# Another opening for a fused attention and soft mixture-of-experts kernel

## The chip, the cores and the metric

The kernel runs on one core of one Trainium2 chip. The metric is the device time of one execution in microseconds (us), the median of the runs shown. Engines are named as in the profile: PE is TensorE's matmuls and PEld its weight loads, DVE is VectorE, ACT is ScalarE, POOL is GpSimd, SP is SyncE, which issues every DMA of this kernel.

## What is computed

Causal attention with a decay over 8 batches and 8 heads, 576 positions of 64 elements each, and then a soft mixture of 8 experts with 4 slots each over the 4608 rows of 512 that the attention gives. All of it in float32:

```python
log_f = np.log(np.clip(f, 0.0001, 1.0))
cum = np.cumsum(log_f, axis=-1)
scores = scale * (q @ k.T) + cum[:, :, :, None] - cum[:, :, None, :]   # -1e9 above the diagonal
x = softmax(scores) @ v                    # heads side by side: 4608 x 512
logits = x @ phi                           # 4608 x 32
slot_input = softmax(logits, axis=0).T @ x
slot_out = relu(slot_input @ w1) @ w2      # by expert
out = softmax(logits, axis=1) @ slot_out
```

## The kernel before

The 64 heads are taken as 32 pairs (g = 0 to 31), head i = 2g + h. For each head TensorE makes the scores twice. `s1` (L211) makes them by query blocks, and `tops` (L224) on VectorE adds the causal mask and takes each row's maximum into a tile MT. The maxima are turned into rows and become an operand of the second pass: `s2` (L260, L261) makes the scores transposed, with the decays and the maxima subtracted by the matmul itself, and `expo` (L267) on ScalarE takes the exponential into PTS. `causal` (L275, L278) on GpSimd cuts the diagonal, `s3` (L295) multiplies by the values, `norm` (L310 to L315) on VectorE divides.

Operands stand in tiles used in rotation, three deep for RAW, WA and YA (index g % 3). Rows 0 to 63 of WA and YA hold k and q rounded to fp32r by ScalarE (`round_k` L165, `round_q` L170). Row 64 of WA holds the cumulated decay rounded, row 96 its remainder, row 97 of YA takes the maxima, and other rows of 64 to 97 hold constants 0, -1 and -8. `dup_k` (L180) and `dup_q` (L184) copy the rounded operands by DMA into WB and YB, where `low_k` (L190) and `low_q` (L195) on GpSimd put the remainders.

The instructions of each engine run in the order in which the program lists them; that order is written out by hand. Waits between engines are put in by the framework from what tiles are read and written. SP issues the DMAs in program order too, and waits before one where its source or target isn't free.

The opening (L480 to L632) does the following. It fetches the decays f of all 64 heads to `fx`, with the two heads of pair 0 once more on partitions 64 and 96 (L488, L489); clamps them on VectorE (L508), takes the logarithm (ACT L509), sums along the row (DVE L510), rounds to `fp` (DVE L512), and puts the rounded rows and remainders of pair 0 into WA[0] (ACT L526, DVE L515). The remainders of all heads are made on GpSimd (L516). Fills with constants stand ahead of it: GpSimd fills rows of WA and YA for n = 0 and 1 (L495 to L498), VectorE fills a tile of ones `fy` (L500), the PSUM tiles `ring` whole (L505) and parts of the PSUM tiles `pv` (`blank`, L283 and L284). `warm` (L477) is a number of matmuls on `fy` or `cs` whose result in ring[0] (columns 0 to 191) is never used. The decays of pair 1 go by DMA from `fp` into WA[1] (L528), those of the later pairs by way of a DRAM tile `cumd` (L571, `load_cum` L175). The constant rows of WA[1] and YA[1] are copied to WA[2] and YA[2] by DMA (L574, L575).

Then `first(i, n, busy)` makes group n of head i's scores, `busy` warm-up matmuls and the maxima. For pair 0 `first_parts` (L538) copies the maxima from MT into a tile `m2` (a view of LG), and `first_rows` turns them (TensorE L545) and copies them into YA[0] (ACT L548). `both(i, n)` is `s2` and `expo`. Heads 0 to 4 are begun in this way, and from pair 1 on the loop (L666) runs; in it each pair makes `s2` of its own two heads, `s1` of the heads three and four further on, and the transposes of X (`px`, L322) of the pair before. In the last pairs and after the loop come the experts; their weights are fetched from L112, one piece a pair from g = 4 on.

Of the kernel before, what the change touches and what calls it, by code (L numbers as in the profile page):

```python
# [62 lines left out]
def attn_softmoe(ctx: ExitStack, tc: tile.TileContext, qk, v, f, phi, w1, w2, cst, out):  # L63
# [454 lines left out]

    for h in range(2):
        round_k(0, h)  # L520
        round_q(0, h)
        dup_k(0, h, h + 1)
        dup_q(0, h, h + 1)
        if h == 0:
            for n in range(2):
                nc.scalar.copy(WA[0][64:65, S * n : S * n + S], fp[64 + 32 * n : 65 + 32 * n, 0:S])  # L526
# [2 lines left out]
    nc.scalar.activation(fin[:, 0:1], ones[:, 0:1], AF.Exp)
    for h in range(2):  # L530
        low_k(h)
        low_q(h)
    nc.gpsimd.memset(YA[2][0:64, :, 0:64].bitcast(F32), 0.0)
    nc.gpsimd.memset(one, -1.0)

    def first_parts(h):

        nc.vector.tensor_copy(m2[h][:, :, 1:2], MT[0][:, NBLK * h : NBLK * h + NBLK].rearrange("p (t o) -> p t o", o=1))  # L538
# [496 lines left out]
```

## Time and profile before

| | us |
|---|---|
| median of 3 runs | 412.54 |
| lowest and highest | 411.88, 413.23 |
| the profiled execution | 411.51 |
| span of the profiled execution, first to last instruction | 409.8 |

| engine | busy us | share of the span |
|---|---|---|
| PE | 384.8 | 94% |
| PEld | 335.9 | 82% |
| DVE | 287.2 | 70% |
| ACT | 256.3 | 63% |
| POOL | 259.0 | 63% |

The profile is one execution. Times in it count from the span's start. A row of a timeline gives start and length in us, the engine, the source line, the operation, the tiles written and read, the shape, and in brackets how long the engine had been idle before it and what ended that. SPq rows are DMA issues: they tell when SP issued a transfer, not when it landed.

### The profile page before, as it was taken

The page shows a single profiled execution, that of the slowest core. Times are in us where ns is not written, and L with a number is a line of the kernel's source. Part 1 is how long each engine was busy: PE and PEld are TensorE (multiplying, and loading weights), DVE is VectorE, ACT ScalarE, POOL GpSimd, SP SyncE. Part 2 cuts the span into 40 slices and gives each one's busy share as a digit, 9 for nine tenths or more (in the row PEclk, how much of TensorE's full clock was granted, in tenths as well). Part 3 has the DMA queues.
Part 4 walks back from the last instruction along what each step waited for, and adds up shares of the span by engine and source line. Part 5 has one row for each costly group of instructions (what it writes and reads, how often), then busy time and mean ns, then how long its engine had stood idle before and what let it go on. Part 6 is the DMA issues. An engine that isn't in the chain of part 4 may idle for free.

```text
span 409.8 us, 15121 instructions
## 1 busy us (share of the span) xinstructions
PE 384.8 (94%) x5841; PEld 335.9 (82%) x5841; DVE 287.2 (70%) x1134; ACT 256.3 (63%) x655; POOL 259.0 (63%) x347
## 2 busy tenths in 40 slices
PE   4779999999999999999999999999999989999990
PEld 4668999999999998999899899999999875444770
DVE  7768777879787977797779687877887544312661
ACT  5657787768686777677767686788775533010551
POOL 9675888777777777787778677877787610020000
PEclk9799999999999999999999999999999999999997
DMA  6556567677867787777777777677766699998798
GB/s 194 140 159 191 153 172 181 202 209 206 243 204 213 211 239 210 204 204 237 204 205 198 207 203 203 203 203 204 202 176 159 219 372 363 386 417 356 241 370 314
DMA packets 34524, 94.02 MB, mean 229 GB/s; under 512 B 4060, under 2 KB 8850, under 8 KB 34452
## 3 DMA queue, kind: packets, MB, share of 16 engines
q1 hardware_dynamic: 34452, 93.06, 73.5%
q8 instruction: 46, 0.75, 0.7%
q14 instruction: 26, 0.21, 0.1%
HBM read 63.93 MB, written 9.73 MB: 180 GB/s over the span
## 4 chain that ended last, share of the span: by engine, by line
PE 79%; DMA 8%; DVE 7%; ACT 3%; issue 1%; SPq 0%; DVEq 0%; ACTq 0%
PE pv L295 22%; PE ring L260 12%; PE s L211 11%; PE ring L261 11%; PE pv L322 4%; DMA RAW<-in_qk 3%; PE pv L888 3%; DVE s L224 3%; PE lg L360 2%; DMA out<-p 2%; PE pv L855 2%; PE ring L855 2%; PE ds L441 2%; DMA p<-in_w 2%; PE more L965 1%
## 5 line engine op out<-in xcount | busy, mean ns | idle before, releaser
L267 ACT ACTIVATE PTS<-ring 128x320 f32<-128x320 f32 (+2 forms) x256 | 119.7, 514 | 62.9 <-PE ring L261 36.9
L224 DVE CUSTOM_DVE_ANT_0 s<-s,mask 128x320 f32<-128x320 f32 (+4 forms) x320 | 137.5, 449 | 8.0 <-PE s L211 3.6
L260 PE MATMUL ring<-YA,WA 98*128 98x320 f32 (+4 forms) x384 | 122.9, 333 | 0.4 <-ACT YA L548 0.4
L261 PE MATMUL ring<-YB,WB 128*128 128x320 f32 (+4 forms) x384 | 111.2, 297 | 0.0
L295 PE MATMUL pv<-V,PTS 128*64 128x65 f32 x3200 | 104.5, 223 | 0.4 <-ACT mr L243 0.3
L211 PE MATMUL s<-WA,YA 97*128 97x288 f32 (+4 forms) x384 | 99.1, 314 | 5.2 <-DVE WA L515 2.2
L295 PEld LDWEIGHTS pv<-V,PTS 128*64 128x64 f32 x3200 | 99.7, 137 | 3.1 <-issue 1.2
L190 POOL TENSOR_TENSOR WB<-RAW,WB 64x576 fp32r<-64x576 f32 x64 | 90.9, 1420 | 5.9 <-DMA WB<-WA 0.7
L195 POOL TENSOR_TENSOR YB<-RAW,YA 64x576 fp32r<-64x576 f32 x64 | 89.5, 1416 | 3.2 <-ACT YA L170 0.7
L260 PEld LDWEIGHTS ring<-YA,WA 98*128 98x128 f32 (+1 forms) x384 | 70.4, 185 | 6.2 <-issue 2.1
L211 PEld LDWEIGHTS s<-WA,YA 97*128 97x128 f32 x384 | 63.7, 192 | 11.3 <-POOL YA L498 2.7
L261 PEld LDWEIGHTS ring<-YB,WB 128*128 128x128 f32 (+1 forms) x384 | 70.5, 184 | 0.0
L275 POOL TENSOR_SCALAR_AFFINE_SELECT PTS<-PTS 128x384 f32<-128x384 f32 x64 | 33.3, 521 | 35.4 <-ACT PTS L267 28.1
L224 DVE DVE_READ_ACCUMULATOR2_ANT MT<- 128x1 f32 x384 | 54.3, 141 | 0.0
L278 POOL TENSOR_SCALAR_AFFINE_SELECT PTS<-PTS 128x128 f32<-128x128 f32 (+1 forms) x128 | 31.3, 265 | 32.2 <-ACT PTS L267 29.8
L165 ACT CAST WA<-RAW 64x576 fp32r<-64x576 f32 x64 | 39.9, 669 | 17.0 <-DMA RAW<-in_qk 16.6
L322 PE MATMUL pv<-cs,X 128*128 128x128 f32 x155 | 42.8, 277 | 0.3 <-DVE X L315 0.2
L224 DVE CUSTOM_DVE_ANT_0 s<-s,mask,MT 128x288 f32<-128x288 f32 x64 | 33.7, 526 | 9.9 <-PE s L211 1.1
L170 ACT CAST YA<-RAW 64x576 fp32r<-64x576 f32 x64 | 40.0, 670 | 0.4
L310 DVE TENSOR_SCALAR rl<-pv 128x5 f32<-128x5 f32 x64 | 10.5, 164 | 34.9 <-PE pv L295 34.9
L315 DVE TENSOR_TENSOR X<-pv,rl 128x320 f32<-128x320 f32 (+1 forms) x65 | 31.5, 486 | 2.4 <-DMA YA<-mr 0.3
L346 ACT COPY XT<-pv 128x128 f32<-128x128 f32 (+1 forms) x124 | 28.6, 292 | 0.0
(208 smaller groups left out, 354.3 us busy)
## 6 DMA issues: line engine op xcount, KB each, us to landing
w<-in_w SPq DMA_DIRECT2D x46, 512.0 KB
RAW<-in_qk SPq DMA_DIRECT2D x31, 576.0 KB
V<-in_v SPq DMA_DIRECT2D x32, 325.0 KB
WB<-WA SPq DMA_DIRECT2D x31, 288.0 KB
YB<-YA SPq DMA_DIRECT2D x31, 288.0 KB
p<-in_w SPq DMA_DIRECT2D x7, 512.0 KB
out<-p SPq DMA_DIRECT2D x6, 512.0 KB
X<-in_w SPq DMA_DIRECT2D x4, 512.0 KB
```

The source lines that it names most:

```text
L165: nc.scalar.copy(WA[g % 3][0:64, S * h : S * h + S], RAW[g % 3][64:128, h])
L170: nc.scalar.copy(YA[g % 3][0:64, h, 64:640], RAW[g % 3][0:64, h])
L190: nc.gpsimd.tensor_tensor(t[0:64], RAW[g % 3][64:128, h], t[64:128].bitcast(F32), op=ALU.subtract)
L195: nc.gpsimd.tensor_tensor(YB[g % 2][64:128, h], RAW[g % 3][0:64, h], YA[g % 3][0:64, h, 64:640].bitcast(F32), op=ALU.subtract)
L211: nc.tensor.matmul(t[:, o : o + w], ya[0:97, h, 128 * blk : 128 * blk + 128], wa[0:97, j0 : j0 + w], start=True, stop=True)
L224: nc.vector.tensor_tensor_reduce(out=t[:, o : o + w], in0=t[:, o : o + w], in1=mask[:, m0 : m0 + w], scale=1.0, scalar=top if n == 3 else ...
L260: nc.tensor.matmul(o, wa[0:98, j0 : j0 + n], ya[0:98, h, 64 + i0 : 64 + i0 + w], start=True, stop=False)
L261: nc.tensor.matmul(o, wb[:, j0 : j0 + n], yb[:, h, i0 : i0 + w], start=False, stop=True)
L267: nc.scalar.activation(PT[i % 2][:, SEG_O[bank] : SEG_O[bank] + at], t[:, 0:at], AF.Exp, scale=0.125)
L275: nc.gpsimd.affine_select(d3, d3, pattern=[[0, 3], [1, 128]], compare_op=ALU.is_ge, fill=0.0, base=0, channel_multiplier=-1)
L295: nc.tensor.matmul(o[64 * u : 64 * u + 64, t, :], PT[i % 2][:, at : at + 64], V[:, g % 2, c, 65 * h : 65 * h + 65], start=(c == 0), stop=( ...
L322: nc.tensor.transpose(pm[:, 0:128], x[:, t, 128 * (p % 2) : 128 * (p % 2) + 128], ident)
```

## The change

- `f` is fetched by three DMAs: all 64 heads, head 0's row broadcast to partitions 64 to 95, and head 1's row to partition 96. The fill of `fx` on VectorE, which the second fetch waited for, is gone.
- The constant rows of index 0 are filled by GpSimd first; those of index 1 by VectorE (WA[1] rows 64 to 95), ScalarE (YA[1], two scaled copies of `fy`, which is 640 wide now) and, behind, GpSimd (the rest).
- `warm` has 8 matmuls instead of 6 and stands ahead of the fills of `ring`; of each ring tile only the corner of 64 partitions and columns 448 to 511 is filled.
- Pair 0's maxima are written straight into `m2`; `first_parts` is gone.
- Pair 0's head 0 is rounded, copied and split before head 1; GpSimd takes head 0's k remainder ahead of the remainders of the decays.
- Pair 1's operands (`load_qk(1)`) are asked for after head 0's copies instead of at the start; pair 2's (`load_qk(2)`) after head 1's copies instead of after pair 1's. The copies of the constant rows to WA[2] and YA[2] stand ahead of the loads of pair 1's decays into WA[1], and these ahead of `cumd` and `load_v(0)`.
- Warm-up matmuls between the first groups are placed otherwise: four behind the first group of head 1, three behind the transposes, none in its later groups.
- Pair 2 is rounded earlier (`round_k(2)` and `round_q(2)` among the groups of heads 1 and 3), `s3(0)` runs in one piece ahead of head 4's first group, and `norm(0)` stands between head 4's groups.

```diff
-WARM = (6, 1)
+WARM = (8, 1)
...
+    m2 = [LG[:, 32 * h : 32 * h + 10].rearrange("p (t c) -> p t c", c=2) for h in range(2)]
...
-            top = MT[g % 3][:, NBLK * h + blk : NBLK * h + blk + 1]
+            top = MT[g % 3][:, NBLK * h + blk : NBLK * h + blk + 1] if g else m2[h][:, blk, 1:2]
...
-    fy = WB[1][:, 0:S].bitcast(F32)
+    fy = WB[1][:, 0:640].bitcast(F32)
...
-    nc.vector.memset(fx[64:97], 1.0)
     nc.sync.dma_start(fx[0 : B * H], f)
-    nc.sync.dma_start(fx[64:97:32], f[0:2])
+    nc.sync.dma_start(fx[64:96], f[0:1].broadcast_to([32, S]))
+    nc.sync.dma_start(fx[96:97], f[1:2])
...
-    for n in range(2):
-        nc.gpsimd.memset(WA[n][64:96].bitcast(F32), 0.0)
-        nc.gpsimd.memset(WA[n][96:98].bitcast(F32), -1.0)
-        nc.gpsimd.memset(YA[n][64:98].bitcast(F32), -8.0)
-        nc.gpsimd.memset(YA[n][0:64, :, 0:64].bitcast(F32), 0.0)
-    load_qk(1)
     nc.vector.memset(fy, 1.0)
...
+    nc.vector.memset(fin, 1.0)
+    nc.scalar.activation(fin[:, 0:1], fin[:, 0:1], AF.Ln)
+    nc.gpsimd.memset(WA[0][64:96].bitcast(F32), 0.0)
+    nc.gpsimd.memset(YA[0][64:98].bitcast(F32), -8.0)
+    nc.gpsimd.memset(WA[0][96:98].bitcast(F32), -1.0)
+    nc.gpsimd.memset(YA[0][0:64, :, 0:64].bitcast(F32), 0.0)
+    nc.vector.memset(WA[1][64:96].bitcast(F32), 0.0)
+    for h in range(2):
+        nc.scalar.mul(YA[1][64:98, h], fy[64:98], -8.0)
+    warm(WARM[0], fy)
     for h in range(2):
         nc.vector.memset(m2[h], -8.0)
     for t in ring:
-        nc.vector.memset(t, 0.0)
+        nc.vector.memset(t[64:128, 448:512], 0.0)
     pvv = [blank(t) for t in pv]
-    warm(WARM[0], fy)
     nc.vector.tensor_scalar(fx, fx, 1e-4, 1.0, op0=ALU.max, op1=ALU.min)
     nc.scalar.activation(fx, fx, AF.Ln)
...
+    nc.gpsimd.memset(WA[1][96:98].bitcast(F32), -1.0)
+    for n in (1, 2):
+        nc.gpsimd.memset(YA[n][0:64, :, 0:64].bitcast(F32), 0.0)
+    nc.gpsimd.memset(one, -1.0)
+    round_k(0, 0)
+    round_q(0, 0)
     nc.vector.tensor_copy(fp[:, 0:S], fz)
     for h in range(2):
+        n, to = 64 + 32 * h, slice(S * h, S * h + S)
+        nc.scalar.copy(WA[0][64:65, to], fp[n : n + 1, 0:S])
+        nc.vector.tensor_tensor(WA[0][96:97, to], fz[n : n + 1], fp[n : n + 1, 0:S].bitcast(F32), op=ALU.subtract)
+    dup_k(0, 0, 1)
+    dup_q(0, 0, 1)
+    load_qk(1)
+    low_k(0)
     nc.gpsimd.tensor_tensor(fp[0 : B * H, S:], fz[0 : B * H], fp[0 : B * H, 0:S].bitcast(F32), op=ALU.subtract)
...
+    low_q(0)
+    round_k(0, 1)
+    round_q(0, 1)
+    dup_k(0, 1, 2)
+    dup_q(0, 1, 2)
+    nc.scalar.activation(fin[:, 0:1], ones[:, 0:1], AF.Exp)
+    low_k(1)
+    low_q(1)
+    load_qk(2)
+    nc.sync.dma_start(WA[2][64:98].bitcast(F32), WA[1][64:98].bitcast(F32))
+    nc.sync.dma_start(YA[2][64:98].bitcast(F32), YA[1][64:98].bitcast(F32))
     for c in range(2):
         nc.sync.dma_start(WA[1][64 + 32 * c : 65 + 32 * c].bitcast(F32), fp[2:4, S * c : S * c + S].bitcast(F32))
...
+    nc.sync.dma_start(cumd.rearrange("h c s -> h (c s)"), fp[0 : B * H].bitcast(F32))
+    load_v(0)
...
     for n in range(4):
         first(0, n, WARM[1])
-    first_parts(0)
+    first(1, 0, 4 * WARM[1])
+    next(r0)
+    warm(3 * WARM[1], cs)
     round_k(1)
-    first(1, 0, WARM[1])
-    next(r0)
     next(r0)
     round_q(1)
-    nc.sync.dma_start(cumd.rearrange("h c s -> h (c s)"), fp[0 : B * H].bitcast(F32))
-    load_v(0)
     dup_k(1)
-    nc.sync.dma_start(WA[2][64:98].bitcast(F32), WA[1][64:98].bitcast(F32))
-    nc.sync.dma_start(YA[2][64:98].bitcast(F32), YA[1][64:98].bitcast(F32))
     dup_q(1)
-    load_qk(2)
     load_cum(2)
-    first(1, 1, WARM[1])
-    first(1, 2, WARM[1])
+    first(1, 1)
+    first(1, 2)
     both(0, 0)
     first(1, 3)
-    first_parts(1)
...
     low_q(2)
+    round_k(2)
...
     load_qk(3)
+    round_q(2)
...
-    round_k(2)
-    round_q(2)
-    s3(0, None, 5)
...
+    s3(0)
+    first(4, 0)
     mturn(1, 1, 2)
     mrows(1, 1, 2)
...
-    s3(0, 5, None)
-    norm(0)
-    first(4, 0)
     first(4, 1)
     s3(1, None, 12)
     first(4, 2)
+    norm(0)
     first(4, 3)
```

## Rows read from the trace of the kernel before

**Rows 1.** Busy time of each engine in stretches of 10 us: start and end, length, then for PE, PEld, DVE, ACT and POOL the busy us and the number of instructions, then the granted TensorE clock (1 is 2.4 GHz), the busy share of the DMA engines, GB/s.

```profile
10.00:20.00 10.00, 7.21 (x33) 6.14 (x32) 7.43 (x23) 6.52 (x11) 6.81 (x7) 0.73 0.51 132
...
40.00:50.00 10.00, 10.00 (x181) 9.55 (x181) 8.32 (x36) 7.48 (x18) 8.32 (x12) 1.00 0.56 155
```

**Rows 2.** The chain of work that ended last, from 0 to 60 us, in order of time: start, us, engine, tile, line.

```profile
10.42 0.33 PE ring L477 x2
...
11.23 0.50 DVE s L224
...
14.38 1.07 DVE LG L538
15.49 1.23 PE ring L545 x5
...
16.96 0.64 PE ring L477 x2
...
31.02 0.52 PE s L211 x2
...
40.13 3.18 PE pv L295 x99
...
49.01 3.18 PE pv L295 x100
```

**Rows 3.** Timeline of the opening, 0 to 16 us, all engines. PE's f32 matmuls are two instructions each.

```profile
2.51 1.56 DVE L505 MEMSET ring<- 128x512 f32 x3
...
3.05 4.21 PE L477 MATMUL ring<-WB 128*128 128x192 f32 x12 [3.05 <-DVE ring L505]
...
4.15 0.11 DVE L283 MEMSET pv<- 64x64 f32 x1
...
4.49 1.05 POOL L495 MEMSET WA<- 32x1152 f32 x1
...
4.63 1.23 DVE L508 TENSOR_SCALAR PTS<-PTS 97x576 f32<-97x576 f32 x1
...
8.57 2.63 DVE L515 TENSOR_TENSOR WA<-PTS 1x576 fp32r<-1x576 f32 x2
8.66 1.92 POOL L516 TENSOR_TENSOR PTS<-PTS 64x576 fp32r<-64x576 f32 x1
...
14.01 1.39 POOL L190 TENSOR_TENSOR WB<-RAW,WB 64x576 fp32r<-64x576 f32 x1
```

**Rows 4.** Who waited for whom from 0 to 45 us: engine, line, whom it waited for, us in total, times, the longest.

```profile
PEld pv L295 <- ACT mr L243: 0.3, 1, 0.3
```

**Rows 5.** The same view for SP's own queue, 0 to 45 us.

```profile
SPq L245 <- DMA YA<-YA: 3.8, 1, 3.8
...
SPq L175 <- DMA WA<-WA: 1.5, 1, 1.5
```

**Rows 6.** Timeline of SP alone: the issues of the copies of the constant rows, of pair 2's and pair 3's operands, of pair 2's decays and of the maxima of head 2.

```profile
11.89 1.35 SPq L528 DMA_DIRECT2D WA<-PTS  x2
...
15.35 0.63 SPq L574 DMA_DIRECT2D WA<-WA  x1
16.03 0.70 SPq L575 DMA_DIRECT2D YA<-YA  x1
...
19.38 1.14 SPq L156 DMA_DIRECT2D RAW<-in_qk  x1
22.08 0.56 SPq L175 DMA_DIRECT2D WA<-cumd  x1
26.48 0.79 SPq L245 DMA_DIRECT2D YA<-mr  x1
...
28.70 0.43 SPq L156 DMA_DIRECT2D RAW<-in_qk  x1
```

**Rows 7.** Timeline from 14 to 50 us, all engines.

```profile
20.68 0.63 PE L211 MATMUL s<-WA,YA 97*128 97x320 f32 x2
...
28.20 1.39 PE L295 MATMUL pv<-V,PTS 128*64 128x65 f32 x40
...
29.05 1.24 ACT L165 CAST WA<-RAW 64x576 fp32r<-64x576 f32 x2 [2.21 <-DMA RAW<-in_qk]
...
32.88 1.25 ACT L165 CAST WA<-RAW 64x576 fp32r<-64x576 f32 x2 [1.17 <-DMA RAW<-in_qk]
...
34.13 0.47 PE L260 MATMUL ring<-YA,WA 98*128 98x448 f32 x1
...
34.91 0.49 DVE L315 TENSOR_TENSOR X<-pv,rl 128x320 f32<-128x320 f32 x1
...
35.46 0.14 PEld L322 LDWEIGHTS pv<-cs,X 128*128 128x128 f32 x1 [0.33 <-DVE X L315]
```

**Rows 8.** Busy time of each engine in shorter stretches, columns as in rows 1.

```profile
14.00:16.00 2.00, 0.51 (x3) 0.34 (x4) 1.90 (x7) 0.07 (x1) 1.91 (x2) 0.67 0.76 166
18.00:20.00 2.00, 2.00 (x8) 1.87 (x7) 0.77 (x3) 1.14 (x3) 0.00 (x0) 0.50 0.17 52
20.00:22.00 2.00, 2.00 (x14) 1.98 (x13) 1.47 (x8) 0.87 (x2) 0.52 (x1) 0.62 0.99 245
```

**Rows 9.** The page: the busy share of the DMA engines in 40 equal slices of the span, in tenths, and the shares of the whole chain by engine.

```profile
DMA  6556567677867787777777777677766699998798
...
PE 79%; DMA 8%; DVE 7%; ACT 3%; issue 1%; SPq 0%; DVEq 0%; ACTq 0%
```

More of the change, by code (lines that the diff above doesn't have):

```diff
@@ L482, in attn_softmoe @@
     fp = PT[1][0:lanes, 0 : 2 * S].bitcast(F32R)
-    fy = WB[1][:, 0:S].bitcast(F32)
+    fy = WB[1][:, 0:640].bitcast(F32)
     st["r", 0] = RAW[0]
-    nc.vector.memset(fin, 1.0)
-    nc.scalar.activation(fin[:, 0:1], fin[:, 0:1], AF.Ln)
-    nc.vector.memset(fx[64:97], 1.0)
     nc.sync.dma_start(fx[0 : B * H], f)
-    nc.sync.dma_start(fx[64:97:32], f[0:2])
+    nc.sync.dma_start(fx[64:96], f[0:1].broadcast_to([32, S]))
+    nc.sync.dma_start(fx[96:97], f[1:2])
     for h in range(2):
@@ L493, in attn_softmoe @@
     nc.sync.dma_start(cs, cst[:, 0:258])
-    for n in range(2):
-        nc.gpsimd.memset(WA[n][64:96].bitcast(F32), 0.0)
-        nc.gpsimd.memset(WA[n][96:98].bitcast(F32), -1.0)
-        nc.gpsimd.memset(YA[n][64:98].bitcast(F32), -8.0)
-        nc.gpsimd.memset(YA[n][0:64, :, 0:64].bitcast(F32), 0.0)
-    load_qk(1)
-    nc.vector.memset(fy, 1.0)
-    m2 = [LG[:, 32 * h : 32 * h + 10].rearrange("p (t c) -> p t c", c=2) for h in range(2)]
+    nc.vector.memset(fy, 1.0)
+    nc.vector.memset(fin, 1.0)
[8 more added lines that the diff above has]
+    warm(WARM[0], fy)
     for h in range(2):
@@ L504, in attn_softmoe @@
     for t in ring:
-        nc.vector.memset(t, 0.0)
+        nc.vector.memset(t[64:128, 448:512], 0.0)
     pvv = [blank(t) for t in pv]
-    warm(WARM[0], fy)
     nc.vector.tensor_scalar(fx, fx, 1e-4, 1.0, op0=ALU.max, op1=ALU.min)
     nc.scalar.activation(fx, fx, AF.Ln)
-    nc.vector.tensor_tensor_scan(fz, fy[0:lanes], fx, 0.0, ALU.mult, ALU.add)
+    nc.vector.tensor_tensor_scan(fz, fy[0:lanes, 0:S], fx, 0.0, ALU.mult, ALU.add)
+    nc.gpsimd.memset(WA[1][96:98].bitcast(F32), -1.0)
+    for n in (1, 2):
+        nc.gpsimd.memset(YA[n][0:64, :, 0:64].bitcast(F32), 0.0)
@@ L512, in attn_softmoe @@
+    nc.gpsimd.memset(one, -1.0)
+    round_k(0, 0)
+    round_q(0, 0)
     nc.vector.tensor_copy(fp[:, 0:S], fz)
     for h in range(2):
-        n = 64 + 32 * h
-        nc.vector.tensor_tensor(WA[0][96:97, S * h : S * h + S], fz[n : n + 1], fp[n : n + 1, 0:S].bitcast(F32), op=ALU.subtract)
-    nc.gpsimd.tensor_tensor(fp[0 : B * H, S:], fz[0 : B * H], fp[0 : B * H, 0:S].bitcast(F32), op=ALU.subtract)
[L519 to L526, printed above, removed]
+        n, to = 64 + 32 * h, slice(S * h, S * h + S)
+        nc.scalar.copy(WA[0][64:65, to], fp[n : n + 1, 0:S])
+        nc.vector.tensor_tensor(WA[0][96:97, to], fz[n : n + 1], fp[n : n + 1, 0:S].bitcast(F32), op=ALU.subtract)
@@ L527, in attn_softmoe @@
     for c in range(2):
         nc.sync.dma_start(WA[1][64 + 32 * c : 65 + 32 * c].bitcast(F32), fp[2:4, S * c : S * c + S].bitcast(F32))
[L529 to L538, printed above, removed]
+    nc.sync.dma_start(cumd.rearrange("h c s -> h (c s)"), fp[0 : B * H].bitcast(F32))
@@ L612, in attn_softmoe @@
     low_q(3)
-    round_k(2)
-    round_q(2)
-    s3(0, None, 5)
+    nc.vector.memset(LG[:, 128:256], -1.0e30)
+    nc.vector.memset(EX[:, 192:256], 0.0)
+    s3(0)
+    first(4, 0)
     mturn(1, 1, 2)
@@ L619, in attn_softmoe @@
     dup_k(2)
-    nc.vector.memset(LG[:, 128:256], -1.0e30)
-    nc.vector.memset(EX[:, 192:256], 0.0)
-    s3(0, 5, None)
-    norm(0)
-    first(4, 0)
     first(4, 1)
```

## The prediction

> **What bounds the kernel now.** I read the trace in four steps. First the busy time in stretches of 10 us [rows 1]: from 40 to 50 us TensorE is busy all the time, from 10 to 20 us 7.21 us of 10, at a mean granted clock of 0.73 of the full 2.4 GHz (the lower level is 1.2). So the loop over the pairs is bound by TensorE, and whatever moves the start of the loop moves the end by as much: the two marks of the loop, 40.13 and 49.01, lie 8.88 us apart [rows 2], a pair of TensorE work, with no wait in it that a shift could fill. Second the chain of waits up to there [rows 2], third the timeline of the opening [rows 3], fourth the waits and the transfers of SP's queue [rows 5, 6]. Three points carry the sum; I call them C, F and L. C is the end of the clamp of the decays (L508), 4.63 + 1.23 = 5.86 [rows 3]. F is the first score matmul of pair 1, the first that reads pair 1's decay rows, at 20.68 [rows 7]. L is the first transposed score matmul of the loop, at 34.13 [rows 7]. So F = C + 14.8 and L = F + 13.45.
>
> **C, the decays.** Before, VectorE reaches the clamp at 4.63 after its fills, the clamp takes 1.23 us, and GpSimd's fill at 4.49 runs until 5.54 [rows 3]; 5.86 - 5.54 = 0.32 us are left, a plausible run of 576 elements, so the clamp stood behind that fill. The change takes most of GpSimd's fills away from there: 1.05 + 1.2 + 1.05 + 0.2 and then 1.05 + 0.6 from 0.8 us on are over near 6 us. It also takes two thirds of VectorE's fills out: three of 128x512 (1.56 us) become three of 64x64 at 0.11 [rows 3].
>
> But it puts the warm-up matmuls ahead of these three fills, into the same PSUM bank as the first (columns 0 to 191 there, 448 to 511 here). Does the fill wait for them? In the trace the value matmuls of head 1, which write columns below 325 of a PSUM tile, wait 0.3 us for ScalarE's copy L243, which reads columns 325 and up of the same tile [rows 4]. So the order is kept by bank, not by column, and the fill waits for all eight matmuls. On VectorE's queue behind it: two fills, four of pv, the clamp, and so every decay. If it were kept by column, the clamp would come about 3 us earlier (a rival, below). The Trainium skill, PSUM — Partial Sum Buffer, section PSUM bank collisions raise a hardware error, speaks against the change here: two engines have to be kept apart on one bank and quadrant even at disjoint columns.
>
> The warm-up starts when the 640-wide ones are there: at 0.52 us for 512 elements (1.56 for three [rows 3]) 0.87 + 0.65 = 1.5 us. Before, twelve instructions took 4.21 us [rows 3], 0.35 each, sixteen then 5.6 us, to 7.1. If the clock rises halfway they go at 0.17 each (the pair at 10.42 in 0.33 us [rows 2]) and end at 5.8. I take 6.5. Then three fills (0.45 with their gaps), the four of pv (4.15 to 4.63, 0.48) and the clamp with GpSimd at rest, 0.32: C = 7.75, between 7.1 and 8.4. First term: **+1.9 us (+1.2 to +2.5)**.
>
> Other edits here cost nothing: the broadcast fetch replaces a fill and is one DMA issue more (0.6 us on SP), over by 2.5 us, long before 6.5; if VectorE came at 4 us, its landing would count. The two scaled copies on ScalarE (0.75 each) fit between the table load and the wait for the clamp.
>
> **From C to the first maxima.** Logarithm, scan, cast and the first difference follow as before; the maxima began at 11.23 [rows 2], C + 5.4. The second difference took 1.87 of the 2.63 us of the pair, since GpSimd's difference (8.66, 1.92 us) ran until 10.58 [rows 3]. After, GpSimd's next reading step waits for a copy through DMA that is issued at C + 1.4 and takes over 2 us, so the second difference runs free: 1.2 us saved, first maxima at C + 4.2. The copy of the maxima that is removed (14.38, 1.07 us [rows 2]) stood behind GpSimd's step at 14.01 that ended at 15.40 [rows 3]; another 1.07 saved. These 2.2 us bring head 0 forward, but not F, as follows.
>
> **F, pair 1's decay rows.** Before, SP loads these two rows (L528) at 11.89 and only then copies the constant rows of WA[1] and YA[1] to WA[2] and YA[2], at 15.35 and 16.03 [rows 6]. After, the two copies come first. The row loads write rows that the first copy reads, so they wait for its landing, and everything queued behind them on SP waits too: the store of the decays, V of pair 0, the copies of pair 1's operands, the decays of pair 2. That such a wait is made the trace shows: the store of maxima into YA[1] stood 3.8 us until the YA copy had landed, at 26.45, and the decays of pair 2 until the WA copy had, at 22.06 [rows 5, 6]. So the copies took 6.7 us and 10.4 us from their issue.
>
> They are slow because few DMA engines carry them: from 18 to 20 us the share is 0.17 of 16 engines and 52 GB/s [rows 8]; 153 KB at 52 GB/s is 2.9 us, the 170 KB of YA 3.3 us, one after the other. The Trainium skill, DMA: Bandwidth & Descriptors, section Why a DMA increments its semaphore by 16 and not by 1, gives the rule, which speaks against this change: the engines are the largest number up to 16 that divides the rows, 2 for 34 rows, always the lowest ones. By it the row loads (2 rows) use the same two engines; it would change the sum by the 3.3 us of the YA copy.
>
> Now in numbers from C, by the rows of each step: operand copies of head 0 are issued at C + 1.4 and C + 2.1, pair 1's operands at C + 2.65 (4.17 us before), head 1's copies at C + 4.7 and C + 5.4, pair 2's operands at C + 5.9, the WA copy at C + 6.4, the YA copy at C + 7.1. An operand load takes 4.2 us (28.70 to 32.88 [rows 6, 7]), so the engines come to the WA copy at C + 9 to C + 10, and it lands at C + 12 to C + 13.2 (6.7 after its issue gives C + 13.1). The row loads are issued then. If they are free of the YA copy they land in 2 us, C + 14.5; behind it at C + 15.4 to C + 17.8. I take the latter, since pair 2's operands, asked for at 19.38 behind the YA copy [rows 6], came only at 29.05, with ScalarE waiting 2.21 us for them [rows 7], 9.7 us where 4.2 do without such a copy ahead: F = C + 16.2. Second term: 16.2 - 14.8 = **+1.4 us (-0.3 to +3.0)**. TensorE would be there sooner: first maxima at C + 4.2, head 0's 3.1 (11.23 to 14.38), transposes 1.23 [rows 2] and their copies, 1.9, three groups of scores 1.5, in all C + 10.7; at half clock, where one warm-up takes 0.64 instead of 0.33 us [rows 2] and the transposes wait for five of them, near C + 15. It idles until F either way.
>
> **From F to L.** Before, head 4's scores start at 31.02, 10.3 us after F, because pair 2's operands came so late [rows 2, 7]. After, they are long there; what is late next is VectorE, whose maxima take 3.1 us a head [rows 2]: heads 2 and 3 end at F + 6.8. TensorE in between makes head 0's 50 value matmuls (40 took 1.39 us [rows 7], 1.75 in all), so head 4 starts at F + 7.2, 3.1 us sooner. Paid back: norm(0), three instructions with 0.49 the largest [rows 7], 0.93 in all, now stands between head 4's maxima, norm(1) behind them, and the transposes of X that waited 0.33 us [rows 7] wait about 1.4. Third term: **-2.0 us (-2.4 to -0.6)**, the last if TensorE's clock is low there.
>
> **Sum.** 1.9 + 1.4 - 2.0 = +1.3 us. The profiled run took 411.51 us with a span of 409.8, 1.03 below the median of 412.54; a shift of the loop applies to both, so 412.54 + 1.3 = **413.8 us**, +0.3%, which is about what a measurement of this kernel can tell from no change.
>
> **The rivals.** (1) The row loads are not held: the WA copy lands before C + 7, or tiles are tracked in a way that I misread. F is then set by TensorE at 18.5 to 22.8, and L = F + 11.4 is 29.9 to 34.2, say 32, 2.1 us sooner: 410.4 us. For it: the copies may run faster where no other transfer stands ahead of them; against: 6.7 and 10.4 us in the trace. (2) The fills are tracked by address: C is near 5, F near 21.2, L 32.6, so 411.0 us; against it stands the wait of [rows 4]. (3) Slower still: TensorE idles up to 5 us ahead of F. In the trace its clock fell in a stretch from 14 to 16 us in which TensorE was busy 0.51 of 2 us, and was back only between 20 and 22 us [rows 8]. If it falls ahead of F, the scores of heads 2 and 3 and the value matmuls (1.75 to 3.5 us) run at half clock: +1.5 to 2 us, 415.6 us; it decides where the granted clock at F is 0.5. (4) The opening moves, but the end doesn't: the last tenths show the DMA engines at 9 and more [rows 9], so the weights could set the end: 412.5 us. Against it: their loads are issued from the same loop, and DMA is 8% of the chain [rows 9].
>
> **How the numbers follow.** Forecast 0.45, rival (1) 0.17, (2) 0.08, (3) 0.17, (4) 0.13. The three terms at their low ends give 411.0, at their high ends 417.4, and hardly all at once; with (2), half of (1) and (3) the range is 410.6 to 416.0. Slower by over 0.3%: (3) and half of the forecast, some more from its upper bounds, 0.43. Faster: (1), part of (2), 0.2. Within: 0.37.
>
> **What would show it.** VectorE's first 64x64 fill starting when the last warm-up matmul ends, and the clamp ending past 7 us, show the first step right; a clamp before 6 us shows it wrong. SP's row loads issued over 4 us after the YA copy, and TensorE idle before pair 1's first scores, show the second. Head 4's scores about 7 us after them and a longer wait of the transposes of X show the third. If the rows land before TensorE asks for them, the prediction is wrong on the fast side.

## The result and the profile after

The changed kernel takes 415.25 us (median of 5 runs, 414.6 to 415.94) where the kernel before takes 412.54; the ratio is 1.0063, with a 95% interval of 1.0035 to 1.0091, so 1.4 to 3.8 us slower. The profiled execution took 414.94 us with a span of 413.2. The line numbers of the changed kernel are 2 higher in the helpers: `s1` is L213, `s2` L262 and L263, `tops` L226, `s3` L297, `expo` L269.

First the timeline of the opening after, as in [rows 3].

```profile
1.65 5.02 PE L479 MATMUL ring<-WB 128*128 128x192 f32 x16 [1.65 <-DVE fin L495]
...
6.76 0.26 DVE L509 MEMSET ring<- 64x64 f32 x3 [3.68 <-PE ring L479]
...
7.46 0.46 DVE L511 TENSOR_SCALAR PTS<-PTS 97x576 f32<-97x576 f32 x1
...
12.34 0.50 DVE L226 CUSTOM_DVE_ANT_0 s<-s,mask 128x320 f32<-128x320 f32 x1 [0.17 <-PE s L213]
```

The fill of ring stands 3.68 us until the last warm-up matmul has ended, and the clamp ends at 7.46 + 0.46 = 7.92. That is C, 2.06 us later than before. The first maxima start at C + 4.42.

SP's issues after, as in [rows 6]: the copies to WA[2] (L542) and YA[2] (L543), pair 1's decay rows (L545), pair 3's operands (L158). Then SP's waits, as in [rows 5].

```profile
14.59 0.71 SPq L542 DMA_DIRECT2D WA<-WA  x1
15.34 0.61 SPq L543 DMA_DIRECT2D YA<-YA  x1
21.43 1.23 SPq L545 DMA_DIRECT2D WA<-PTS  x2
...
33.07 0.43 SPq L158 DMA_DIRECT2D RAW<-in_qk  x1
```

```profile
SPq L545 <- DMA WA<-WA: 5.4, 1, 5.4
```

Busy time in stretches of 2 us, columns as in rows 1 (start and end, length, PE, PEld, DVE, ACT, POOL, granted clock, DMA share, GB/s).

```profile
18.00:20.00 2.00, 2.00 (x15) 1.93 (x12) 0.53 (x2) 1.70 (x4) 1.32 (x1) 1.00 0.13 53
20.00:22.00 2.00, 0.89 (x6) 0.62 (x4) 1.46 (x6) 1.45 (x4) 0.42 (x1) 1.00 0.12 52
22.00:24.00 2.00, 0.00 (x0) 0.00 (x0) 0.00 (x0) 0.00 (x0) 0.10 (x1) 0.78 0.22 74
24.00:26.00 2.00, 0.68 (x3) 0.71 (x4) 0.00 (x0) 0.00 (x0) 0.00 (x0) 0.50 0.97 234
26.00:28.00 2.00, 2.00 (x13) 1.66 (x13) 0.98 (x4) 0.60 (x2) 0.19 (x1) 0.50 1.01 291
28.00:30.00 2.00, 2.00 (x8) 1.87 (x8) 1.40 (x5) 1.97 (x4) 1.58 (x3) 0.51 0.33 73
```

The row loads are held 5.4 us, until 21.43, for the WA copy. From 18 to 22 us the DMA share is 0.12 to 0.13 of 16 engines, which is the work of two engines, at 52 GB/s: those that make the copies. From 22 to 24 us TensorE, VectorE and ScalarE do nothing at all. In this rest the granted clock falls, and it is 0.50 to 0.51, the lower level of 1.2 GHz, from 24 to 30 us.

The timeline further on, as in [rows 7]: F, head 4's first scores, L, ScalarE's rounding of pair 3, the transposes of X.

```profile
25.32 0.77 PE L213 MATMUL s<-WA,YA 97*128 97x320 f32 x2 [4.44 <-DMA WA<-PTS]
...
33.95 0.50 PE L213 MATMUL s<-WA,YA 97*128 97x320 f32 x2
...
37.32 0.47 PE L262 MATMUL ring<-YA,WA 98*128 98x448 f32 x1
...
38.65 1.24 ACT L167 CAST WA<-RAW 64x576 fp32r<-64x576 f32 x2 [3.76 <-DMA RAW<-in_qk]
...
39.35 0.33 PE L324 MATMUL pv<-cs,X 128*128 128x128 f32 x1 [0.78 <-DVE X L317]
```

F is at 25.32 (C + 17.4, before C + 14.8), with TensorE waiting 4.44 us for the row loads. L is at 37.32 (F + 12.0, before F + 13.45). But the shift is not over at L: ScalarE waits 3.76 us for pair 3's operands, and it has to round them before it goes on with the loop's exponentials. The chain of waits shows the place from which the loop runs evenly, the first long row of value matmuls; I call its start M.

```profile
22.11 2.97 DMA WA<-PTS
...
45.52 3.18 PE pv L297 x84
54.40 3.18 PE pv L297 x94
```

M is at 45.52, before at 40.13 [rows 2], 5.39 us later; the next pair follows 8.88 later in both. From M to the end of the span it is 413.2 - 45.52 = 367.7 after, 409.8 - 40.13 = 369.7 before.

### The profile page after: what moved, and what is told of

Read it like the earlier page. It is cut to its first block, busy times and chain, and to the rows that moved or that the text cites. A ratio compares the mean times of both kernels' runs of the same rounds, so it can differ in the third digit from the quotient of the medians.

```text
span 413.2 us, 15143 instructions
## 1 busy us (share of the span) xinstructions
PE 387.0 (94%) x5853; PEld 339.8 (82%) x5853; DVE 283.6 (69%) x1132; ACT 258.0 (62%) x657; POOL 255.1 (62%) x345
## 4 chain that ended last, share of the span: by engine, by line
PE 87%; DVE 4%; DMA 3%; ACT 2%; issue 1%; POOL 0%; DVEq 0%; ACTq 0%
PE pv L297 24%; PE ring L262 13%; PE s L213 12%; PE ring L263 12%; PE pv L324 4%; PE lg L362 3%; PE pv L890 3%; PE ring L479 2%; PE pv L857 2%; DMA out<-p 2%; PE ring L857 2%; PE ds L443 2%; PE more L967 1%; ACT PTS L269 1%; PE pv L236 1%
## 5 line engine op out<-in xcount | busy, mean ns | idle before, releaser
L269 ACT ACTIVATE PTS<-ring 128x320 f32<-128x320 f32 (+2 forms) x256 | 119.9, 514 | 63.5 <-PE ring L263 37.8
L226 DVE CUSTOM_DVE_ANT_0 s<-s,mask 128x320 f32<-128x320 f32 (+4 forms) x320 | 137.4, 448 | 15.1 <-PE s L213 10.7
L262 PE MATMUL ring<-YA,WA 98*128 98x320 f32 (+4 forms) x384 | 122.6, 332 | 1.2 <-ACT PTS L269 1.2
L263 PE MATMUL ring<-YB,WB 128*128 128x320 f32 (+4 forms) x384 | 111.1, 297 | 0.0
L213 PE MATMUL s<-WA,YA 97*128 97x288 f32 (+4 forms) x384 | 100.3, 318 | 9.3 <-DVE WA L527 4.9
L297 PE MATMUL pv<-V,PTS 128*64 128x65 f32 x3200 | 104.3, 223 | 0.6 <-ACT mr L245 0.6
L297 PEld LDWEIGHTS pv<-V,PTS 128*64 128x64 f32 x3200 | 99.6, 137 | 3.2 <-issue 1.2
L213 PEld LDWEIGHTS s<-WA,YA 97*128 97x128 f32 x384 | 64.9, 196 | 14.5 <-ACT WA L526 5.1
L262 PEld LDWEIGHTS ring<-YA,WA 98*128 98x128 f32 (+1 forms) x384 | 70.2, 184 | 7.1 <-issue 2.1
L263 PEld LDWEIGHTS ring<-YB,WB 128*128 128x128 f32 (+1 forms) x384 | 70.5, 183 | 0.0
L226 DVE DVE_READ_ACCUMULATOR2_ANT MT<- 128x1 f32 x372 | 52.7, 142 | 0.0
L226 DVE CUSTOM_DVE_ANT_0 s<-s,mask,MT 128x288 f32<-128x288 f32 x62 | 32.6, 526 | 9.2 <-PE s L213 0.5
```

Of the source, the lines that this page charges most:

```text
L213: nc.tensor.matmul(t[:, o : o + w], ya[0:97, h, 128 * blk : 128 * blk + 128], wa[0:97, j0 : j0 + w], start=True, stop=True)
L226: nc.vector.tensor_tensor_reduce(out=t[:, o : o + w], in0=t[:, o : o + w], in1=mask[:, m0 : m0 + w], scale=1.0, scalar=top if n == 3 else ...
L262: nc.tensor.matmul(o, wa[0:98, j0 : j0 + n], ya[0:98, h, 64 + i0 : 64 + i0 + w], start=True, stop=False)
L263: nc.tensor.matmul(o, wb[:, j0 : j0 + n], yb[:, h, i0 : i0 + w], start=False, stop=True)
L269: nc.scalar.activation(PT[i % 2][:, SEG_O[bank] : SEG_O[bank] + at], t[:, 0:at], AF.Exp, scale=0.125)
L297: nc.tensor.matmul(o[64 * u : 64 * u + 64, t, :], PT[i % 2][:, at : at + 64], V[:, g % 2, c, 65 * h : 65 * h + 65], start=(c == 0), stop=( ...
```

## The experiments

Each was timed beside the kernel before on the same chip; a ratio is the experiment's time over that kernel's, with its 95% interval in brackets. They come from several sessions, in which the median of the kernel before lay between 412.54 and 412.99 us. So medians from different sessions compare to a few tenths of a us.

**Row loads ahead of the copies.**

```diff
+    for c in range(2):
+        nc.sync.dma_start(WA[1][64 + 32 * c : 65 + 32 * c].bitcast(F32), fp[2:4, S * c : S * c + S].bitcast(F32))
     nc.sync.dma_start(WA[2][64:98].bitcast(F32), WA[1][64:98].bitcast(F32))
     nc.sync.dma_start(YA[2][64:98].bitcast(F32), YA[1][64:98].bitcast(F32))
-    for c in range(2):
-        nc.sync.dma_start(WA[1][64 + 32 * c : 65 + 32 * c].bitcast(F32), fp[2:4, S * c : S * c + S].bitcast(F32))
```

> The changed kernel with one edit: the loads of pair 1's decay rows stand ahead of the copies of the constant rows to WA[2] and YA[2]. Theory (the row loads wait for the copy, and that alone holds pair 1's first scores): the row loads are issued near 15, right after GpSimd's remainders, and land before 18; pair 1's first scores start when TensorE has ended head 0's exponent scores, near 20.9 in place of 25.3, and the first long row of value matmuls in the loop near 41 in place of 45.5. If all of it reaches the end, 415.25 - 4.4 = 410.9 us, with some 2 us given back later 413. Rival (the two rows are slow for another reason, behind pair 2's operands): they land after 22, the scores start after 23, and the time is 414 to 415.3.

Measured: 416.89 us, ratio 1.0106 [1.0082, 1.013]. The timeline:

```profile
20.32 0.40 PE L213 MATMUL s<-WA,YA 97*128 97x320 f32 x2
...
30.10 0.57 SPq L177 DMA_DIRECT2D WA<-cumd  x1
30.16 0.87 ACT L269 ACTIVATE PTS<-ring 128x448 f32<-128x448 f32 x2 [6.15 <-issue]
...
31.75 1.41 POOL L192 TENSOR_TENSOR WB<-RAW,WB 64x576 fp32r<-64x576 f32 x1 [9.27 <-DMA WB<-WA]
```

The first half of the theory holds: F is at 20.32 and TensorE does not wait there. The second half falls: M is at 46.12, later still, and the time is no better. GpSimd now waits 9.27 us for the copy of pair 1's operands (`dup_k(1)`, which stood behind the copies of the constant rows before the edit too, but is now issued while they still run). ScalarE idles 6.15 us (its row names no releaser), and pair 2's decays are asked for at 30.10. The granted clock is 0.50 from 26 to 36 us, TensorE having rested from 26 to 30. The order on SP chose who stands behind the copies.

**Fills ahead of the warm-up.**

```diff
-    warm(WARM[0], fy)
     for h in range(2):
         nc.vector.memset(m2[h], -8.0)
     ...
     pvv = [blank(t) for t in pv]
+    warm(WARM[0], fy)
```

> The changed kernel with one edit: the warm-up matmuls stand behind the fills of ring and pv again, as in the kernel before. Theory (the clamp is late because the fill of ring waits for the warm-up, and everything up to pair 1's scores follows the clamp): the clamp ends near 4.3 in place of 7.9, pair 1's first scores start 17.4 later as before, near 21.7, and the value matmuls of the loop near 41.9; 411.6 us if it reaches the end whole, 413.7 with 2 us given back. Rival (the copies set pair 1's scores, whenever the clamp ends): the clamp is as early, but the scores stay past 24 and the time within 1 us of 415.25.

Measured: 415.28 us, ratio 1.0061 [1.0041, 1.0081], the same as with the change whole. From the timeline and the waits:

```profile
3.85 0.53 DVE L511 TENSOR_SCALAR PTS<-PTS 97x576 f32<-97x576 f32 x1
...
22.14 0.77 PE L213 MATMUL s<-WA,YA 97*128 97x320 f32 x2 [6.76 <-DMA WA<-PTS]
```

```profile
ACT WA L167 <- DMA RAW<-in_qk: 4.4, 2, 4.2
```

C is at 4.38 and F at 22.14, each within half a microsecond of the theory, but M is at 44.31 where the theory gave 41.9: ScalarE stands 4.2 us for pair 3's operands, and the granted clock was 0.50 from 20 to 26 us, having fallen while TensorE waited its 6.76 us (it was low once more, 0.58 and 0.56, from 40 to 44 us). Of 3.5 us gained at C, 1.2 were left at M and none can be measured at the end.

**Both edits.**

> The changed kernel with both edits. Theory (the two costs add up): the clamp ends near 4.3, pair 1's first scores start near 17 to 18, the value matmuls of the loop near 37 to 38, some 3 us sooner than in the kernel before (40.13); if the end follows whole, 407.5 us, if transfers later in the loop hold it at a time of their own, 410.5 to 412.5. Rival (one hides the other): no better than the better of the two alone.

Measured: 412.91 us, ratio 1.0008 [0.999, 1.0025], the same as before. Together they give 2.3 us, alone nothing: the time does not add up from C and F. F is at 15.20, 5.5 us ahead of the kernel before, and M at 42.80. The waits say who took it:

```profile
POOL WB L192 <- DMA WB<-WA: 13.2, 2, 10.8
```

Again GpSimd waits 10.8 us for pair 1's operand copy, which is issued while the copies of the constant rows still occupy two engines. The granted clock is 0.50 or little more from 24 to 34 us, so the wait and the clock behind it share what is lost.

**A pure delay.**

```diff
+    warm(32, cs)
     for g in range(1, NG):
```

> The kernel before with 32 warm-up matmuls more right ahead of the loop over the pairs, 32 x 0.164 = 5.25 us of TensorE and nothing else. It asks how much of a shift of the loop reaches the end. Theory (in the kernel before some pairs wait for operands whose transfers keep a time of their own, so a later loop waits less): the first pairs are 5.3 us later, the end 3.0 to 3.5 us, 415.7 us. Rival (the waits seen in that one trace are chance, or move with the loop): the end is 5.3 us later, 417.8 us.

Measured: 422.27 us, ratio 1.023 [1.0193, 1.0267]. I had mis-costed the delay: 0.33 us is one warm-up, of two instructions, so 32 are 10.7 us.

```profile
34.38 10.67 PE L477 MATMUL ring<-cs 128*128 128x192 f32 x64
```

M moved by 10.36 us to 50.49, the span by 8.0, and the median by 9.5 (from 412.81). Between the two traces 2.4 us are taken up later, about the 2 that the theory gave back; by the medians it is only 0.9. The delayed kernel's own executions lie between 419.18 and 423.53 us, and the profiled one, 419.49, is among its fastest. So most of a shift reaches the end, and how much comes back is left open by this run.

**The copies split.**

```diff
-    nc.sync.dma_start(WA[2][64:98].bitcast(F32), WA[1][64:98].bitcast(F32))
-    nc.sync.dma_start(YA[2][64:98].bitcast(F32), YA[1][64:98].bitcast(F32))
+    for a, z in ((64, 96), (96, 98)):
+        nc.sync.dma_start(WA[2][a:z].bitcast(F32), WA[1][a:z].bitcast(F32))
+    for a, z in ((64, 96), (96, 98)):
+        nc.sync.dma_start(YA[2][a:z].bitcast(F32), YA[1][a:z].bitcast(F32))
```

> The changed kernel with one edit: each copy of the constant rows to WA[2] and YA[2] is made as two, 32 rows and 2 rows, in place of one of 34 rows; the order on SP stays, with two issues more (1.3 us). Theory (34 rows go over two DMA engines only, and whatever is queued on those two behind them is late; 32 rows spread over all 16, like the 64-row operand copies that land in 2.1 us): the copies land within 3 us of their issue in place of 6.8, the row loads are issued near 18.5 in place of 21.4 and land near 20.5 in place of 25; pair 1's first scores start near 21, the value matmuls of the loop near 40.5 in place of 45.5, and the time is 410.5 to 412. Rival (the copies are slow because of what stands ahead of them, pair 2's operands, not because of the engines they use): they land after 20.5, the scores start past 24, and the time stays within 1 us of 415.25.

Measured: 412.89 us, ratio 1.001 [0.9981, 1.0039], 2.4 us better than the change. SP's issues, and the stretches:

```profile
15.04 1.36 SPq L543 DMA_DIRECT2D WA<-WA  x2
16.45 1.19 SPq L545 DMA_DIRECT2D YA<-YA  x2
20.49 1.27 SPq L547 DMA_DIRECT2D WA<-PTS  x2
```

```profile
18.00:20.00 2.00, 2.00 (x16) 1.82 (x15) 0.00 (x0) 0.91 (x3) 1.72 (x2) 1.00 0.64 156
20.00:22.00 2.00, 1.65 (x11) 1.34 (x9) 1.62 (x6) 2.00 (x5) 0.00 (x0) 1.00 0.02 5
```

Both were partly right. The stretch in which only two engines work is gone: 0.64 of the engines are busy from 18 to 20 us, 0.02 after that. But the row loads are released only 0.9 us sooner (20.49); that the split copies now stand behind pair 2's operands on all engines would explain it and was not tested. F comes to 23.01, with 1.36 us of waiting. M is at 43.00; the granted clock, 1.00 at F, was 0.50 from 38 to 40 us.

**The copies split, and the fills ahead.**

> The same split copies, and the fills of ring and pv ahead of the warm-up. Theory (the clamp and the two clogged DMA engines are the whole loss, and add up): the clamp ends near 4.4, pair 1's first scores start near 17.5, nobody waits over 3 us for the operand copies of pair 1, and the value matmuls of the loop start near 36.5, 3.6 us before those of the kernel before; 408.5 to 410 us. Rival (something else then sets the loop's start, pair 3's operands, which are asked for behind the maxima of head 2): the value matmuls past 38.5, 411 us.

Measured: 411.51 us, ratio 0.9965 [0.9947, 0.9983]. C is at 4.38, F at 18.88, M at 42.37: the rival holds. The chain of waits:

```profile
26.65 7.28 DMA RAW<-in_qk
```

Pair 3's operands, asked for at 26.65 (behind the maxima of head 2, V of pair 1 and phi), take 7.28 us, and ScalarE waits 6.31 us for them.

**Pair 3's operands sooner, on top.**

```diff
     load_cum(2)
+    load_qk(3)
 ...
-    load_qk(3)
```

> The changed kernel with the split copies, the fills ahead of the warm-up, and one edit more: pair 3's operands are asked for right behind the load of pair 2's decays, in place of behind the maxima of head 2, V of pair 1 and phi. In the run without this edit ScalarE waited 6.3 us for them, issued at 26.65 and landed at 34, while the DMA engines had stood nearly still from 24 to 26. Theory (the request comes too late): issued near 21.5, landed near 27, ScalarE waits under 1 us, the value matmuls of the loop start near 38 in place of 42.4, and the time falls from 411.5 to 407.5 to 409. Rival (between 26 and 36 all 16 DMA engines are busy, so the same bytes end at the same time in any order): pair 2's or pair 4's operands or V are late in their place, the value matmuls past 41, the time within 1 us of 411.5.

Measured: 407.78 us, ratio 0.9889 [0.9864, 0.9914]. SP's issue of pair 3's operands:

```profile
22.32 0.87 SPq L158 DMA_DIRECT2D RAW<-in_qk  x1
```

M is at 38.22, and ScalarE's longest wait for operands is 0.3 us. The theory holds: one line moved is worth 3.7 us by the medians, 3.1 by the ratios to the kernel before (the run without it is from another session).

**The row loads ahead, on top of that.**

> The same kernel with the loads of pair 1's decay rows ahead of the four copies. Theory (with copies that are quick the order matters little for what stands behind them, and pair 1's scores gain the 3.5 us for which TensorE waited): pair 1's first scores near 15.5 in place of 18.9; the value matmuls of the loop near 36.5; 1 to 2 us less than the kernel beside it. Rival (the copies come 2 us later and hold pair 2's decays, and what sets the loop's start is pair 3's operands): no difference over 0.7 us.

Measured: 408.02 us, ratio 0.9891 [0.9873, 0.991]. F is at 15.51 in place of 19.68, M at 37.66 in place of 38.22: the rival. Four microseconds at F are worth nothing that can be measured. TensorE is busy only 0.52 of 2 us from 22 to 24 us here, and the granted clock is 0.50 or little more from 22 to 28.

**Parts alone in the kernel before.** The split copies, and nothing of the change:

> The kernel before with the split copies and nothing else of the change. Theory: the operands of pair 2 land near 25 in place of 29, ScalarE does not wait 2.2 us for them, and the value matmuls of the loop start near 38 in place of 40.13; 410.5 us. Rival (the wait for pair 2's operands was covered by VectorE's maxima): within 0.7 us of the kernel before.

Measured: 408.15 us, ratio 0.988 [0.9857, 0.9903]. ScalarE's two waits for operands in [rows 7], 2.21 and 1.17 us, became these:

```profile
25.16 1.24 ACT L165 CAST WA<-RAW 64x576 fp32r<-64x576 f32 x2
...
30.66 1.25 ACT L165 CAST WA<-RAW 64x576 fp32r<-64x576 f32 x2 [2.85 <-DMA RAW<-in_qk]
```

SP's issue of pair 2's load:

```profile
19.36 0.59 SPq L156 DMA_DIRECT2D RAW<-in_qk  x1
```

Pair 2's load is issued when it was before (19.36, before 19.38 [rows 6]), and its operands are rounded at 25.16 without waiting, in place of 29.05. M is at 37.53, and the time falls by more than the theory said, 4.8 us. With pair 3's operands sooner as well:

> The kernel before with the split copies and pair 3's operands asked for right behind the load of pair 2's decays. With the split copies alone it took 408.15 us. Theory (transfers that are asked for too late set the start of the loop there too): ScalarE's next wait for operands goes, the value matmuls of the loop start near 36.5 in place of 37.5; 407 us. Rival (VectorE's maxima set it there): within 0.7 us of 408.15.

Measured: 407.89 us, ratio 0.9891 [0.9866, 0.9916], M at 36.57. The trace agrees with the theory, the time with the rival: 0.3 us is no difference that these runs can tell. And with one part of the change in addition, maxima written where they are turned:

```diff
-            top = MT[g % 3][:, NBLK * h + blk : NBLK * h + blk + 1]
+            top = MT[g % 3][:, NBLK * h + blk : NBLK * h + blk + 1] if g else m2[h][:, blk, 1:2]
...
-    first_parts(0)
...
-    first_parts(1)
```

> The kernel before with the split copies, pair 3's operands asked for sooner, and one part of the change: pair 0's maxima are written straight where they are turned, so that the two copies of 1.07 us (L538) are gone. In the run without this part the chain of waits up to 30 us is VectorE's, and the first copy stands on it (14.37 to 15.44). Theory (a cut on that chain reaches the loop): the value matmuls of the loop start near 35.5 in place of 36.6, the time falls by 1 us from 407.9 to about 406.9. Rival (the operands of pairs 2 and 3, or TensorE, are late next by as much): within 0.5 us of 407.9.

Measured: 406.14 us, ratio 0.9837 [0.9802, 0.9872], the lowest median of all; M is at 35.49, 1.08 us sooner than without this part, and the span 1.4 us shorter. The theory holds in the trace. By the medians it is 1.75 us, but the two runs are from different sessions and the intervals of their ratios overlap. In the run without it its chain of waits held the copy:

```profile
14.37 1.07 DVE LG L538
```

**The kernel before, a second time.**

> The kernel before itself, once more with a profile, to tell what of its trace is chance. In its first trace the loop lost 2.1 us between 160 and 250 us to operand loads that came late, and the kernels with a later start lost less there. If these waits belong to the kernel's own timing, the second trace shows them again, 1.5 us or more; if they are chance, they are elsewhere or gone, and the span moves with them.

One run: 413.57 us, span 411.9. Its chain, and the stretches where it differs from the first trace:

```profile
19.38 9.83 DMA RAW<-in_qk
...
43.01 3.18 PE pv L295 x84
```

```profile
28.00:30.00 2.00, 0.54 (x20) 0.40 (x14) 0.85 (x3) 0.77 (x2) 1.28 (x1) 1.00 0.77 218
30.00:32.00 2.00, 0.72 (x5) 0.51 (x6) 0.25 (x1) 1.88 (x4) 0.77 (x1) 1.00 0.77 249
32.00:34.00 2.00, 2.00 (x30) 1.66 (x32) 1.64 (x9) 0.90 (x2) 2.00 (x2) 0.66 0.12 47
34.00:36.00 2.00, 2.00 (x27) 1.88 (x28) 1.21 (x8) 1.59 (x3) 0.01 (x1) 0.50 1.03 200
36.00:38.00 2.00, 2.00 (x9) 1.90 (x9) 1.42 (x5) 0.98 (x2) 0.00 (x0) 0.50 0.83 173
```

ScalarE's rounding of pairs 2 and 3 in it:

```profile
29.23 1.24 ACT L165 CAST WA<-RAW 64x576 fp32r<-64x576 f32 x2 [3.44 <-DMA RAW<-in_qk]
...
33.10 1.24 ACT L165 CAST WA<-RAW 64x576 fp32r<-64x576 f32 x2 [1.22 <-DMA RAW<-in_qk]
```

M is at 43.01, 2.9 us later than in the first trace of the same kernel, though F is 0.8 sooner (19.92). The operands do not make the difference: pairs 2 and 3 are rounded at 29.23 and 33.10, in the first trace at 29.05 and 32.88 [rows 7]. TensorE did little from 28 to 32 us, waiting for pair 2's operands, and its granted clock then fell to 0.50. In the first trace it was busier from 28 to 30 (1.59 of 2 us), and the clock stayed at 1.00. From head 4's first scores to M it is 11.80 us here (31.21 to 43.01) and was 9.11 there (31.02 to 40.13), nearly the whole 2.9 us.

The granted clock at the start of a trace needs care. In the first trace it was low from 14 to 22 us [rows 8]; in the second it reads 1.00 from 10 to 20 us, yet a warm-up matmul's two instructions take as long there as in the first trace at 0.50 (first row: the second trace; second row: the first trace). So TensorE was slow there in both.

```profile
16.75 0.84 PE L477 MATMUL ring<-cs 128*128 128x192 f32 x2
...
16.76 0.84 PE L477 MATMUL ring<-cs 128*128 128x192 f32 x2
```

From M to the end it is 368.9 us, and 369.7 in the first trace. TensorE idles 0.4 us between 160 and 240 us here, 1.0 in the first trace. That is below the 1.5 us that were to show these later waits again, so they are chance in the main. The larger chance is in the opening itself.

The marks of the profiled runs side by side (us; M from the chain of waits, F from the timeline):

| kernel | C | F | M | span | span - M | median |
|---|---|---|---|---|---|---|
| before, two traces | 5.86, 5.86 | 20.68, 19.92 | 40.13, 43.01 | 409.8, 411.9 | 369.7, 368.9 | 412.54 |
| changed | 7.92 | 25.32 | 45.52 | 413.2 | 367.7 | 415.25 |
| rows first | 7.68 | 20.32 | 46.12 | 414.6 | 368.5 | 416.89 |
| fills first | 4.38 | 22.14 | 44.31 | 412.3 | 368.0 | 415.28 |
| both | 4.38 | 15.20 | 42.80 | 410.7 | 367.9 | 412.91 |
| before, delayed | 5.87 | 20.70 | 50.49 | 417.8 | 367.3 | 422.27 |
| split | 8.39 | 23.01 | 43.00 | 411.6 | 368.6 | 412.89 |
| split, fills | 4.38 | 18.88 | 42.37 | 410.5 | 368.1 | 411.51 |
| split, fills, pair 3 sooner | 4.37 | 19.68 | 38.22 | 406.4 | 368.2 | 407.78 |
| the same, rows first | 4.45 | 15.51 | 37.66 | 406.3 | 368.6 | 408.02 |
| before, split | 5.86 | 19.28 | 37.53 | 406.0 | 368.5 | 408.15 |
| before, split, pair 3 sooner | 5.86 | 18.38 | 36.57 | 405.1 | 368.5 | 407.89 |
| the same, maxima in place | 5.86 | 17.30 | 35.49 | 403.7 | 368.2 | 406.14 |

The end follows M, 367.3 to 369.7 us behind it in all fourteen traces: from the earliest M to the latest it is 15.0 us, and the spans of these two differ by 14.1. It follows F much less: with F between 19.2 and 20.8 us, M lies anywhere from 37.5 to 50.5 (46.1 without the delayed kernel).

## Why the prediction was right, and where it was off

The sign was right and the time lies in the range; the forecast's 413.8 was 1.4 us low. That the time came so near is partly luck: the three terms measured sum to +3.2 at L in place of +1.3, a fourth loss of 2.2 us was not in the sum, and the median moved by only 2.7.

**C, +1.9.** Measured +2.06, by the mechanism named: the 64x64 fill starts when the last warm-up matmul has ended. The clamp with GpSimd at rest took 0.46 us, not the 0.32 worked out. Rival (2) falls. But as a term of the sum it was over-valued. With the fills put back, C and F come 3.5 and 3.2 us sooner and the time stays at 415.28; only with the row loads moved as well does it count. The prediction laid C, F and L in one series; pair 3's operands run beside them.

**F, +1.4.** Measured 17.4 - 14.8 = +2.6, inside the bounds of -0.3 to +3.0. The copy released the row loads at C + 13.5 (13.1 worked out), and they landed at 25.08, C + 17.2 (15.4 to 17.8 worked out). Their last step in the chain is 2.97 us long here and 1.68 in the same kernel with the copies split, so the YA copy in their way cost about 1.3 us. Rival (1) falls. That the wait is real is shown by moving the row loads ahead: it disappears. That it costs what it lasts is refuted by the same run, 416.89 us. What costs is two DMA engines that are busy for some 7 us with the copies; in the orders tried something stood behind them, and the step "F later, so the loop later" failed. The Trainium skill, DMA: Bandwidth & Descriptors, section Why a DMA increments its semaphore by 16 and not by 1, gives the cause in the number of rows: 2 engines for 34 rows and 16 for 32. The traces agree, with 0.12 to 0.13 of 16 engines from 18 to 22 us for copies of 34 rows, and with copies of 32 no such stretch: 0.64 from 18 to 20 us and 0.02 after that.

**F to L, -2.0.** Measured 12.0 - 13.45 = -1.45. Head 4's scores came at F + 8.6 (7.2 worked out, 10.3 before): pair 2's operands were there, as said, but heads 2 and 3 were made at the lower clock until 30 us. The transposes of X waited 0.78 in place of 0.33 us, less than the 1.4 feared for `norm(0)`.

**The copies are no cost of the change alone.** They slow both kernels. Split, they take 4.8 us off the kernel before and 2.4 off the changed one, and the changed kernel is then 4.7 us slower in place of 2.7 (412.89 against 408.15). With the fills ahead and pair 3's load moved as well, both kernels come out alike, 407.78 and 407.89. So what the change itself costs, once the copies are quick, is the fills and pair 3's late load, and the rest of it gains nothing that these runs can tell.

**What the sum did not have.** After L another 2.2 us are lost up to M (37.32 to 45.52 is 8.20, before 34.13 to 40.13 is 6.00), while ScalarE waits 3.76 us for pair 3's operands. The granted clock is 1.00 from 30 us on, so this is not the clock. Their load stands on SP behind the store of head 2's maxima, so the late F delays it too: 33.07 in place of 28.70 [rows 6]. The prediction took L for the start of the loop and listed every DMA that SP was held from up to pair 2's decays, not this one, four issues further. That moving this load matters is shown by the run in which it alone was moved (3.7 us by the medians), in a kernel in which the copies were split and the fills put back; in the changed kernel as it stands it was not moved alone.

**What came back.** Four terms make 2.06 + 2.58 - 1.45 + 2.20 = 5.39, the shift of M; the span grew by 3.4 and the median by 2.7. Between M and the end 2.0 come back. Of these, 1.0 is idle time of TensorE between 160 and 240 us, which the first trace of before has and the changed kernel does not; the prediction's "no wait in it that a shift could fill" holds for the pair that it looked at, not for the whole loop. Whether a later start fills such waits or chance does is not settled: the second trace of before has 0.4 there. The trace on which the sum was made weighs more: the second trace has M at 43.01, and against that the change's M is 2.5 us later, close to the medians. Rival (4) falls as well, since the delay moved the median by 9.5. The prediction's step that one execution's F and L stand for the kernel was the weakest one: between two traces of one kernel, where the clock fell moved M by 2.9 us.

**Rival (3).** Its condition, a granted clock of 0.5 at F, was met: TensorE rested from 22 to 24 us and ran at 0.50 or 0.51 from 24 to 30. But its price was not borne out where it was put: F to L came out 0.55 us above the forecast, not 1.5 to 2, and the 50 value matmuls ran at a granted clock of 1.00 (from 32.4 us, 1.66 us). So that 415.25 lies near its 415.6 is chance. What the clock alone costs was not isolated; the split copies in the changed kernel remove the rest and the low clock at F together and give back 2.4 us, with a low clock from 38 to 40 us in their place. Nor was `norm(0)` tried in its old place. The gain of the maxima written in place was hidden where something else was late: put into the kernel before with the transfers out of the way, the same edit brings M 1.08 us forward (407.89 to 406.14 us by the medians).

## What to carry to other kernels

Find the first place from which the work runs evenly and judge an opening by that mark alone, in more than one trace; waits that disappear ahead of it are no gain until it moves. Before moving a DMA in a queue, look at how many DMA engines carry it: here a slow transfer on two engines delayed the wide transfers behind it, and the order chose which, so make it wide (32 + 2 rows for 34 took 4.8 us off the kernel before) before thinking of the order. And follow a queue past the moved instruction to the last load that the steady work needs, not only to the first that waits.

## What the runs showed of the hardware

- Two copies of 34 rows split into 32 + 2 made a difference of 4.8 us in the kernel before, though SP issues two transfers more. Whole, they kept two of 16 DMA engines busy at 52 GB/s; a load issued behind them at the same time (19.38 and 19.36 us) was rounded at 29.05 us with the copies whole and at 25.16 with them split. In the changed kernel with both edits GpSimd waited 10.8 us for a 64-row copy behind them.
- The same kernel with the same opening reached M at 40.13 and 43.01 us; the recorded stretches of low granted clock lay from 14 to 22 us in one trace and from 32 to 40 in the other, TensorE having been busy 0.51 of 2 us where it began in the one, and 0.54 and 0.72 of 2 us ahead of it in the other. That alone makes a single trace a poor base for terms of 1 or 2 us.
- The granted clock read 1.00 at the start of the second trace while a warm-up matmul took 0.84 us at 16.75 us, as long as at 0.50 in the first trace (16.76 us). Durations of like matmuls are the check.
